# A routing table ordered by slots instead of by experts, in a fused scan and two-layer expert kernel

## The chip, the cores and the metric

One core of one Trainium2 chip runs the whole program in one launch. The metric is the device time in microseconds of an execution; the number given for a kernel is the median of its runs.

## The reference, cut to what matters

```python
# q, k, v, a_re, a_im: [4, 8, 768, 48]
for t in range(768):                          # complex decay, |a| at most 0.999
    S_re, S_im = ar*S_re - ai*S_im + outer(k[t], v[t]), ar*S_im + ai*S_re
    y[t] = q[t] @ S_re
x = y as [N=3072, D=384]                      # tokens x (heads*48)
# first expert layer, 8 experts, F=1024; only tokens with x @ w_skip > 0
e = argmax(x @ w_gate);  g = softmax(x @ w_gate)[e]
x = x + g * relu(x @ w1[e]) @ w2[e]           # the others keep x
# second expert layer, 8 experts, all tokens, no residual
l = norm(x) @ norm(emb).T / tau;  e = argmax(l);  g = softmax(l)[e]
out = g * relu(x @ w1b[e]) @ w2b[e]
```

## The kernel before, in words

**Stages.** The scan goes over 24 chunks of 128 tokens (`chunk`), some 36 to 250 us after the start. The first expert layer (`moe1`) then computes 8 experts with 256 slots each, the second (`moe2`) 8 experts with at most 448. An expert's part of a layer is: fetch token rows by their numbers (`gather`, an indirect DMA of GpSimd into `xg`, line 1003), transpose them (`x_part`, TensorE line 927, evicted to `x` by ScalarE at 933 and VectorE at 934), first matmul (`h_part`, 958), second (`o_part`, 990), and store the output rows by their numbers (`finish`, indirect DMAs of GpSimd: into `xd` at 1044 in the first layer, into `out` at 1239 in the second).

**The routing table.** A token finds its place in `route`: from its logits VectorE makes a one-hot of the expert, a matmul with `SU` (strictly upper triangle and ones) counts the tokens ahead of it, `cnt` holds the count so far and the expert's base, and the sum is the number of a table row. GpSimd then scatters one row per token into the DRAM table by indirect DMA (line 739). A row has W = 17 floats, 68 bytes: 8 logits, the token's number less N, 8 logits. There are two tables, `tab[0]` and `tab[1]`, called lanes; a row is written in one of them, and the other holds zeros there. In either, a layer has its region, and in the region the rows lie by experts: expert e's slot s is row e*N + s. At the start, GpSimd fills the used part with zeros in eight DMAs (line 799); a slot that stays empty thus reads as token N, whose row in `xd` is zero.

**Reading back.** `slots` (line 764) reads 128 slots of every expert from both lanes: SyncE issues two DMAs (767), one into `ts1f` or `ts2f`, one into `LANE`; VectorE adds the two (768) and, in the first layer, makes the indices `ts1i` (770). Of a row 9 columns are wanted, the number and the layer's logits: 36 bytes. As experts lie apart, each slot of each expert is a piece of its own:

```python
return tab[lane][r*E*N : (r+1)*E*N, :].rearrange("(e r) c -> e r c", e=E)[:, a:b, c0:c1]
```

The reads are: one slot tile of expert 0 alone (`early`, "A") and one more ("E") during the scan; the other seven experts' two slot tiles at the scan's end (`moe1`, "ts" 0 and 1); during the first layer the first two slot tiles of the second ("ts2", "A"), for its first expert; and at the end of the first layer all four again (`moe2`), for the other experts. There the order of the experts is found on the chip, by how many tokens they have: `select` (1153) picks for the p-th the rows of its expert out of `ts2f` by a multiply with the one-hot `OH` (1158) and a reduction over the experts (1160) into one of three tiles `F2`, and makes the indices `ts2i` (1161).

**Order.** `Plan` writes each engine's instructions in an order of its own: a list scheduler with a cost for each operation, due times, and dependences by keys (the lists `r` and `w`). An engine works through its queue in that order, SyncE and GpSimd with their DMAs too, and an instruction that waits holds those behind it. After a DMA the planner counts its flight and a charge on top, `more`: for a read of the table 1.2 us. The early reads are ordered behind the scatters that they need by keys.

Of the kernel before, what the change touches and what calls it, by code (L numbers as in the profile page):

```python
# [9 lines left out]
F32 = mybir.dt.float32  # L10
# [268 lines left out]
def kernel(  # L279
# [41 lines left out]
    F2 = [cp.tile([P, 4, E + 1], F32, name=f"F2{i}") for i in range(3)]  # L321
    wrs = cp.tile([P, NPR, 113], F32, name="wrs")
# [4 lines left out]
    LANE = cp.tile([P, E * 4, E + 1], F32, name="LANE")  # L327
# [251 lines left out]
    def chunk(k):  # L579
# [13 lines left out]
        def half(hh):  # L593
# [3 lines left out]
            def w_():  # L597
# [6 lines left out]
                [("ps", hh)], [("wm", k % 2, hh)], D0 - 2)  # L604
# [50 lines left out]
        if ui == UN[u] - 1:  # L655
# [15 lines left out]
            if u == LATE_U - 1:  # L671
                slots(ts1, lambda x: x[:, 1:2, :], lambda lane: region(lane, 0, P, 2 * P)[0].rearrange("p (o c) -> p o c", o=1),
                      sum(tabs, []) + [("tabB", lane) for lane in range(2)], ("ts", "E"), d2 + 4)
            plan.bias = 0.0

    def reserve(c, slots):
# [3 lines left out]
            cnt[:, c : c + 1], pb, float(c * N + slots), ident[:, 0:1], ALU.max, ALU.mult), [("ps7", 3)], ["cnt"])  # L680
# [3 lines left out]
    def route(nm, n, nr, lg, klg, sel, ksel, c0, pay, kpay, inval, pcol, due, late=(), pt0=0):  # L684
# [51 lines left out]
        dve(C, lambda: V.tensor_tensor(cc, cc, cn, op=ALU.add), [k("cn")], ["cnt"])  # L736
        for i in range(n):
# [4 lines left out]
                [("ix", nm)] + klg + kpay + span(["ti"], range(2), (0, E // 2), [lane]), [("tab", nm, i)] + ([("tabB", lane)] if late else []), due, (f"t{lane}", "all"), 1.3, 1.2)  # L742
# [835 lines left out]
```

## Time and profile before

| | |
|---|---|
| median of 3 runs | 703.61 us (701.12 to 706.31) |
| profiled execution, its own time | 706.19 us |
| its span from first to last instruction | 704.3 us |
| mean granted clock of TensorE | 0.958 of full speed |
| TensorE busy (matmuls) | 622.6 us, 88% of the span, 4740 instructions |
| VectorE, ScalarE, GpSimd busy | 459.5, 403.1 and 189.9 us |
| DMA packets | 52007, of them 22909 under 512 bytes |

All rows come from one profiled execution. PE is TensorE's matmuls, PEld its weight loads, DVE is VectorE, ACT ScalarE, POOL GpSimd, SP SyncE; PEq or SPq is an engine's queue. A line as L958 is a line of the kernel; x stands for a count. What stands in brackets in a timeline is the time in which the engine was idle just before the instruction, and what ended it. Times in rows are microseconds from the start of the span, lengths microseconds.

### The profile page before, as it was taken

How to read it: one execution, taken by the hardware profiler on the slowest of the kernel's cores; microseconds unless marked ns; L12 is line 12 of the kernel's file. 1: busy time of each engine (PE TensorE's matmuls, PEld its weight loads, DVE VectorE, ACT ScalarE, POOL GpSimd, SP SyncE). 2: the span in 40 equal slices, each digit the busy share in tenths (PEclk: the TensorE clock that was granted, in tenths of full speed). 3: DMA queues.
4: the chain of work that ended last, by engine and by line, in shares of the span. 5: the costliest groups of instructions: out<-in, count | busy, mean ns of one | idle time of the engine just before them, and what ended most of it. 6: DMA issues, size and time to landing. Idle time of an engine off the chain costs nothing.

```text
span 704.3 us, 12899 instructions
## 1 busy us (share of the span) xinstructions
PE 622.6 (88%) x4740; PEld 599.5 (85%) x4740; DVE 459.5 (65%) x1058; ACT 403.1 (57%) x695; POOL 189.9 (27%) x221
## 2 busy tenths in 40 slices
PE   0088979999979996899999999849999999999994
PEld 0088978889969985899999999749999999999994
DVE  4989888899875553667776657528755636365240
ACT  6977895987856542555555434027553545545340
POOL 5111011025536226122232033443140412111101
PEclk9997898999989999799999999959999999999998
DMA  9858579899556877666554231494653434123001
GB/s 271 315 161 253 204 139 287 251 207 217 127 142 161 271 238 235 209 201 216 167 157 124 87 108 24 84 336 157 226 195 106 148 113 136 37 89 119 23 10 36
DMA packets 52007, 115.91 MB, mean 165 GB/s; under 512 B 22909, under 2 KB 27139, under 8 KB 49250
## 3 DMA queue, kind: packets, MB, share of 16 engines
q1 hardware_dynamic: 41282, 84.50, 38.9%
q0 software_dynamic: 10656, 30.53, 16.1%
q8 instruction: 39, 0.64, 0.4%
q14 instruction: 30, 0.25, 0.1%
HBM read 83.30 MB, written 14.09 MB: 138 GB/s over the span
## 4 chain that ended last, share of the span: by engine, by line
PE 66%; issue 10%; DMA 9%; DVE 6%; ACT 4%; POOL 2%; another core or an unknown queue 1%; SPq 1%; POOLq 0%; DVEq 0%; ACTq 0%
PE PS L958 25%; PE PS L990 24%; PE PS L599 3%; DMA ST<-QK 3%; PE PS L626 3%; PE PS L927 3%; PE PS L436 2%; DMA xd<-XT 2%; PE PS L635 2%; PE PS L646 2%; POOL tab L739 1%; DMA LANE<-tab 1%; PE PS L1061 1%; PE PS L610 1%
## 5 line engine op out<-in xcount | busy, mean ns | idle before, releaser
L990 PE MATMUL PS<-w,h 128*128 128x384 f32 (+1 forms) x1032 | 190.7, 339 | 0.9 <-ACT h L962 0.9
L958 PE MATMUL PS<-x,w 128*128 128x256 f32 (+4 forms) x1152 | 183.3, 317 | 0.0
L990 PEld LDWEIGHTS PS<-w,h 128*128 128x128 f32 (+1 forms) x1032 | 176.2, 184 | 4.1 <-ACT h L962 1.2
L958 PEld LDWEIGHTS PS<-x,w 128*128 128x128 f32 x1152 | 174.9, 194 | 2.1 <-issue 0.4
L962 ACT ACTIVATE h<-PS 128x256 fp32r<-128x256 f32 (+5 forms) x136 | 58.1, 428 | 102.9 <-PE PS L958 92.1
L966 DVE SCALAR_TENSOR_TENSOR h<-PS,h 128x256 fp32r<-128x256 f32 (+4 forms) x184 | 67.4, 390 | 58.7 <-ACT h L962 54.4
L1239 POOL DMA_INDIRECT out<-o,ts2i x30 | 29.9, 997 | 169.7 <-ACT o L1233 123.4
L908 DVE TENSOR_TENSOR w<-r,w 128x768 fp32r<-128x768 f32 x64 | 58.8, 950 | 10.9 <-ACT w L907 7.4
L934 DVE TENSOR_TENSOR x<-PS,x 128x256 fp32r<-128x256 f32 (+4 forms) x48 | 22.6, 484 | 59.4 <-ACT x L933 46.9
L933 ACT CAST x<-PS 128x256 fp32r<-128x256 f32 (+4 forms) x48 | 19.7, 427 | 70.8 <-PE PS L927 49.0
L599 PE MATMUL PS<-ST 96*128 96x128 f32 x384 | 55.1, 291 | 5.4 <-DVE WM L602 3.0
L902 DVE TENSOR_TENSOR w<-r,w 128x1024 fp32r<-128x1024 f32 x45 | 53.3, 1222 | 6.6 <-ACT w L901 5.4
L907 ACT CAST w<-r 128x768 fp32r<-128x768 f32 x64 | 51.0, 833 | 9.5 <-PE PS L990 4.4
L599 PEld LDWEIGHTS PS<-ST 96*128 96x128 f32 x384 | 49.0, 201 | 8.2 <-DVE WM L602 3.6
L436 PE MATMUL PS<-cst 128*128 128x128 f32 x308 | 47.6, 301 | 5.8 <-DVE cs L816 4.3
L436 PEld LDWEIGHTS PS<-cst 128*128 128x128 f32 x308 | 43.3, 214 | 6.7 <-DVE cs L816 4.4
L739 POOL DMA_INDIRECT tab<-LG,ixa x24 | 33.8, 1407 | 47.2 <-DVE ixa L731 13.1
L602 DVE TENSOR_TENSOR WM<-PS,cst 128x512 f32<-128x512 f32 x48 | 32.3, 680 | 20.8 <-PE PS L599 15.3
L901 ACT CAST w<-r 128x1024 fp32r<-128x1024 f32 x45 | 44.6, 1048 | 0.3 <-DMA r<-in_w1a 0.3
L546 POOL DMA_DIRECT2D ST<-QK x50 | 25.4, 516 | 68.6 <-DVE QK L534 66.7
L1003 POOL DMA_INDIRECT xg<-xd,ts2i x30 | 33.1, 1104 | 34.5 <-PE PS L958 10.6
L1044 POOL DMA_INDIRECT xd<-o,ts1i x16 | 17.4, 1088 | 91.5 <-DVE o L1041 59.4
(210 smaller groups left out, 985.2 us busy)
## 6 DMA issues: line engine op xcount, KB each, us to landing
r<-in_w1a SPq DMA_DIRECT2D x24, 512.0 KB
r<-in_w2a SPq DMA_DIRECT2D x32, 384.0 KB
r<-in_w1b SPq DMA_DIRECT2D x24, 512.0 KB
r<-in_w2b SPq DMA_DIRECT2D x32, 384.0 KB
RI<-in_ri SPq DMA_DIRECT2D x6, 1152.0 KB
QK<-in_qk SPq DMA_DIRECT2D x6, 1152.0 KB
ST<-PR SPq DMA_DIRECT2D x12, 432.0 KB
ST<-QK POOLq DMA_DIRECT2D x12, 432.0 KB
```

What stands on the lines that cost most here:

```text
L436: nc.tensor.matmul(PS[7][:, 384:512], lhsT=ident, rhs=maskT, start=True, stop=True)
L599: nc.tensor.matmul(wt[:, h % 4, :], lhsT=st(1, h), rhs=st(0, h), start=True, stop=True)
L739: pool(0.2, lambda i=i, lane=lane: nc.gpsimd.indirect_dma_start(out=tab[lane][:, :], out_offset=IO(ap=ix[:, i : i + 1].bitcast(U32), axis= ...
L901: act(F, lambda s=s: nc.scalar.copy(T["w1"][q % 2][0][s], T["r1"][q % 2][s]), [("r1", q % 2, j), "L"], [k + (0,)])
L902: dve(F, lambda s=s: nc.vector.tensor_tensor(T["w1"][q % 2][1][s], T["r1"][q % 2][s], T["w1"][q % 2][0][s].bitcast(F32), op=ALU.subtract), ...
L907: act(2 * DM, lambda s=s: nc.scalar.copy(T["w2"][0][s], T["r2"][s]), [("r2", j)], [k + (0,)])
L908: dve(2 * DM, lambda s=s: nc.vector.tensor_tensor(T["w2"][1][s], T["r2"][s], T["w2"][0][s].bitcast(F32), op=ALU.subtract), [("r2", j), k + ...
L958: nc.tensor.matmul(ph, lhsT=l, rhs=r, start=(i == 0), stop=(i == len(seq) - 1))
L962: act(w, lambda f=f, ph=ph: nc.scalar.activation(T[name][:, f, o0 : o0 + w], ph, AF.Relu), [("ps", f % 3), "w" if name == "hA" else "L"], ...
L966: dve(b - a, lambda f=f, ph=ph, a=a, b=b, o=o: nc.vector.scalar_tensor_tensor(T[name][:, f, o : o + b - a], ph[:, a - c0 : b - c0], 0.0, T ...
L990: nc.tensor.matmul(po if n == P else po[0 : 2 * stride], lhsT=x, rhs=w[:, f, :], start=(f == 0 and i == 0), stop=(f == NF - 1 and i == len ...
L1003: pool(0.6, lambda: nc.gpsimd.indirect_dma_start(out=T["xg"][s][0:n, :], out_offset=None, in_=xd[0:rows, :], in_offset=IO(ap=idx.bitcast(U ...
```

## The change

The table's rows are ordered by slots: slot s of expert e is row s*8 + e of its layer's region, so that the eight experts' rows of one slot lie together, 8 x 68 = 544 bytes. Slot numbers are multiplied by 8 throughout: in `SU`, the counts, the bases, the limits and the capacities; `SU` takes one multiply more for it.

The reads of 128 slots take whole rows of a slot, all 17 columns: 544 bytes for the second layer (`slots2`), 476 (seven experts) for the first. `LANE` and `ts2f` have 17 columns for it; `LANE` shares its memory with the routing weights `wrs`, and in the first layer both lanes are read into it. Only the two reads of expert 0 alone in the scan keep pieces of 36 bytes (`slots1`, into the new `LE`). The add takes the 9 wanted columns. `select` works on the same number of elements at another step. The three `F2` tiles lie in the columns of the causal mask `maskT`, with a new key "mask" between the mask's readers and the reductions; the matmuls that keep TensorE's clock up (`warm`) read the identity instead. The zero fill writes contiguous runs (1088 and 1904 bytes for each of 64 partitions). The planner's charge after a read is 0.8 us instead of 1.2.

The diff, without lines that only change an index or an offset in the same way:

```diff
-    F2 = [cp.tile([P, 4, E + 1], F32, name=f"F2{i}") for i in range(3)]
-    wrs = cp.tile([P, NPR, 113], F32, name="wrs")
+    F2 = [maskT[:, 4 * (E + 1) * i : 4 * (E + 1) * (i + 1)].rearrange("p (t c) -> p t c", t=4) for i in range(3)]
+    lane = cp.tile([P, E * 4 * W], F32, name="lane")
+    wrs = lane[:, 0 : NPR * 113].rearrange("p (a c) -> p a c", a=NPR)
...
-    LANE = cp.tile([P, E * 4, E + 1], F32, name="LANE")
+    LANE = lane.rearrange("p (i c) -> p i c", c=W)
+    LE = cp.tile([P, 2, E + 1], F32, name="LE")
...
-            nc.tensor.matmul(PS[7][:, 384:512], lhsT=ident, rhs=maskT, start=True, stop=True)
+            nc.tensor.matmul(PS[7][:, 384:512], lhsT=ident, rhs=ident, start=True, stop=True)
...
-                [("ps", hh)], [("wm", k % 2, hh)], D0 - 2)
+                [("ps", hh), "mask"], [("wm", k % 2, hh)], D0 - 2)
...
-                slots(ts1, lambda x: x[:, 1:2, :], lambda lane: region(lane, 0, P, 2 * P)[0].rearrange("p (o c) -> p o c", o=1),
-                      sum(tabs, []) + [("tabB", lane) for lane in range(2)], ("ts", "E"), d2 + 4)
+                slots1(1, P, sum(tabs, []) + [("tabB", lane) for lane in range(2)], ("ts", "E"), d2 + 4)
...
-        dve(C, lambda: V.tensor_tensor(cc, cc, cn, op=ALU.add), [k("cn")], ["cnt"])
+        dve(C, lambda: V.scalar_tensor_tensor(cc, cn, float(E), cc, ALU.mult, ALU.add), [k("cn")], ["cnt"])
...
-    def region(lane, r, a, b, c0=None, c1=None):
-        c0, c1 = (r * E, r * E + E + 1) if c0 is None else (c0, c1)
-        return tab[lane][r * E * N : (r + 1) * E * N, :].rearrange("(e r) c -> e r c", e=E)[:, a:b, c0:c1]
-
-    def slots(t, view, src, ks, key, due, kf=()):
-        parts = [view(x) for x in t["l"]]
+    def region(lane, r, a, b):
+
+        return tab[lane][r * E * N : (r + 1) * E * N, :].rearrange("(s e) c -> s e c", e=E)[a:b]
+
+    def slots(f, parts, src, i, ks, key, due, kf=()):
+
         for lane in range(2):
-            dma(0.2, lambda lane=lane: nc.sync.dma_start(parts[lane], src(lane)), ks, [(key, lane), *kf], due, (f"t{lane}", "read"), more=1.2)
-        dve(math.prod(parts[0].shape[1:]), lambda: nc.vector.tensor_tensor(view(t["f"]), parts[0], parts[1], op=ALU.add), [(key, 0), (key, 1)], [(key, 2), *kf], due)
-        if t is ts1:
-            dve(16, lambda: nc.vector.tensor_scalar(view(t["i"]), view(t["f"])[..., t["c"] : t["c"] + 1], float(N), None, ALU.add), [(key, 2)], [key], due)
-
-    def slot_tiles(nm, n):
-        t = {"f": cp.tile([P, n, E + 1], F32, name=f"{nm}f"), "c": 0 if nm == "ts2" else E}
-        t["l"] = [t["f"], LANE[:, 0:n]]
-        for x in t["l"] if nm == "ts2" else ():
-            nc.gpsimd.memset(x, 0.0)
+            dma(0.2, lambda lane=lane: nc.sync.dma_start(parts[lane], src(lane)), ks, [(key, lane), *kf], due, (f"t{lane}", "read"), more=0.8)
+        o = E if i is None else 0
+        x, y = (p[..., o : o + E + 1] for p in parts)
+        dve(math.prod(f.shape[1:]), lambda: nc.vector.tensor_tensor(f, x, y, op=ALU.add), [(key, 0), (key, 1)], [(key, 2), *kf], due)
+        if i is not None:
+            dve(16, lambda: nc.vector.tensor_scalar(i, f[..., E : E + 1], float(N), None, ALU.add), [(key, 2)], [key], due)
+
+    def slots1(c, a, ks, key, due):
+
+        f = ts1["f"][:, c * E : c * E + 1]
+        slots(f, (f, LE[:, c : c + 1]), lambda lane: region(lane, 0, a, a + P)[:, 0:1, 0 : E + 1], ts1["i"][:, c * E : c * E + 1], ks, (key[0], key[1]), due)
+
+    def slots2(t, n, key, due):
+        f, x = (x[0:n, t * E : t * E + E] for x in (ts2["f"], LANE))
+        slots(f[..., E:], (f, x), lambda lane: region(lane, 1, t * P, t * P + n), None, sum(tabs, []), key, due, [("F", t)])
+
+    def slot_tiles(nm, n, w):
+        t = {"f": cp.tile([P, n, w], F32, name=f"{nm}f")}
...
-        for r, e, lane in itertools.product((0, 1), (0, E // 2), range(2)):
-            n = (CAP1, CAP2)[r] // 64
-            pool(0.4, lambda r=r, e=e, lane=lane, n=n: nc.gpsimd.dma_start(
-                region(lane, r, 0, 64 * n, 0, W)[e : e + E // 2].rearrange("e (p j) c -> p e j c", p=64),
-                zero[:, 0 : E // 2 * n * W].rearrange("p (e j c) -> p e j c", e=E // 2, j=n)), [("S", 0)], [("ti", r, e, lane)], due)
-        dve(P, lambda: nc.vector.tensor_tensor(SU[:, 0], maskT, ident, op=ALU.subtract), (), ["su"], due)
-        dve(P, lambda: nc.vector.tensor_copy(SU[:, 1], ones), (), ["su"], due)
+        for r, x, lane in itertools.product((0, 1), (0, 1), range(2)):
+            n = E * (CAP1, CAP2)[r]
+            part = tab[lane][r * E * N : r * E * N + n, :].rearrange("(x p j) c -> x p (j c)", x=2, p=64)[x]
+            pool(0.4, lambda part=part: nc.gpsimd.dma_start(part, zero[:, 0 : part.shape[1]]), [("S", 0)], [("ti", r, x, lane)], due)
+        dve(P, lambda: nc.vector.tensor_tensor(SU[:, 0], maskT, ident, op=ALU.subtract), ["mask"], ["su"], due)
+        dve(P, lambda: nc.vector.tensor_scalar(SU[:, 0], SU[:, 0], float(E), None, ALU.mult), (), ["su"], due)
+        dve(P, lambda: nc.vector.tensor_scalar(SU[:, 1], ones, float(E), None, ALU.mult), (), ["su"], due)
...
-    ts1, ts2 = slot_tiles("ts1", E * NT1), slot_tiles("ts2", E * 4)
+    ts1, ts2 = slot_tiles("ts1", E * NT1, E + 1), slot_tiles("ts2", E * 4, W)
+    nc.gpsimd.memset(ts2["f"], 0.0)
...
-            slots(ts1, lambda x, t=t: x.rearrange("p (e t) c -> p e t c", e=E)[:, 1:, t, :],
-                  lambda lane, t=t: region(lane, 0, t * P, (t + 1) * P)[1:].rearrange("e p c -> p e c"),
-                  sum(tabs, []), ("ts", t), M0 - 5)
+            f, *x = (x[:, o + t * E + 1 : o + (t + 1) * E] for x, o in ((ts1["f"], 0), (LANE, 0), (LANE, nt * E)))
+            slots(f, x, lambda lane, t=t: region(lane, 0, t * P, (t + 1) * P)[:, 1:], ts1["i"][:, t * E + 1 : (t + 1) * E], sum(tabs, []), ("ts", t), M0 - 5)
...
-                        slots(ts2, lambda x, a=a: x.rearrange("p (e t) c -> p e t c", e=E)[:, :, a],
-                              lambda lane, a=a: region(lane, 1, a * P, a * P + P).rearrange("e p c -> p e c"),
-                              sum(tabs, []), ("ts2", "A", a), due + 20, [("F", a)])
+                        slots2(a, P, ("ts2", "A", a), due + 20)
...
-        src, tmp = (x.rearrange("p (e t) c -> p t c e", e=E)[:, 2 * h : 2 * h + 2] for x in (ts2["f"], LANE))
+        src, tmp = (x.rearrange("p (t e) c -> p t c e", e=E)[:, 2 * h : 2 * h + 2, E:] for x in (ts2["f"], LANE))
         f, V = F2[p % 3][:, 2 * h : 2 * h + 2], nc.vector
         oh = OH[:, p, :].rearrange("p (a b e) -> p a b e", a=1, b=1).to_broadcast([P, 2, E + 1, E])
         dve(250, lambda: V.tensor_tensor(
             tmp, src, oh, op=ALU.mult), kin + [("oh2", min(p, 1))], [("tmp", h)], due)
-        dve(240, lambda: V.tensor_reduce(f, tmp, axis=AX.X, op=ALU.add), kin + [("tmp", h)], [("f2", p % 3, h)], due)
+        dve(240, lambda: V.tensor_reduce(f, tmp, axis=AX.X, op=ALU.add), kin + [("tmp", h)], [("f2", p % 3, h), "mask"], due)
...
-        slots(ts1, lambda x: x[:, 0:1, :], lambda lane: region(lane, 0, 0, P)[0].rearrange("p (o c) -> p o c", o=1),
-              sum(tabs[:3], []), ("ts", "A"), M0 - 20)
+        slots1(0, 0, sum(tabs[:3], []), ("ts", "A"), M0 - 20)
...
-            slots(ts2, lambda x, t=t, n=n: x.rearrange("p (e t) c -> p e t c", e=E)[0:n, :, t, :],
-                  lambda lane, t=t, n=n: region(lane, 1, t * P, t * P + n).rearrange("e p c -> p e c"),
-                  sum(tabs, []), ("ts2", t), M1 - 5, [("F", t)])
+            slots2(t, n, ("ts2", t), M1 - 5)
...
-    cf[:, -P:] = i + P
+    cf[:, -P:] = E * (i + P)
     w8[:] = np.arange(E, 0, -1)
-    base = np.arange(2 * E) * N
+    base = np.concatenate([np.arange(E), E * N + np.arange(E)])
     first[0] = [*base, BIG]
     bia[:] = [math.log(2e-6), SHIFT, -SHIFT, math.pi / 2]
-    lims[:] = base + np.repeat([CAP1, 0], E)
+    lims[:] = base + np.repeat([E * CAP1, 0], E)
     ulim[:] = [U_MAX if g in SQA else U_MAX * U_MAX for g in range(B * TH) for _ in PARTS.get(g, (0,))]
     iota[:] = np.arange(E)
-    caps[:] = CAPS
+    caps[:] = E * np.array(CAPS)
```

## Rows read from the trace of the kernel before

**Rows 1.** The page's chain that ended last, by engine.

```profile
PE 66%; issue 10%; DMA 9%; DVE 6%; ACT 4%; POOL 2%; another core or an unknown queue 1%; SPq 1%; POOLq 0%; DVEq 0%; ACTq 0%
```

**Rows 2.** Busy time (xcount): PE, PEld, DVE, ACT, POOL; clock, DMA, GB/s.

```profile
250.00:292.00 42.00, 32.97 (x233) 31.59 (x231) 20.91 (x74) 17.48 (x40) 18.99 (x18) 0.88 0.78 232
...
292.00:427.00 135.00, 135.00 (x1000) 134.55 (x998) 90.90 (x204) 70.83 (x131) 31.59 (x30) 1.00 0.48 147
...
427.00:490.00 63.00, 50.64 (x343) 48.33 (x343) 37.18 (x167) 21.40 (x60) 27.65 (x31) 0.86 0.53 159
...
490.00:704.30 214.30, 204.84 (x1151) 197.62 (x1149) 104.92 (x257) 101.38 (x207) 40.97 (x41) 0.99 0.31 105
```

**Rows 3.** Waits, 436 to 470: sum, count, longest.

```profile
ACT x L933 <- remote: 17.6, 1, 17.6
...
PE PS L927 <- DVE x L934: 11.0, 1, 11.0
```

**Rows 4.** Timeline of SyncE, scan's end: start, us, issue.

```profile
232.81 0.43 SPq L1195 DMA_DIRECT2D o<-in_cf  x1
...
261.62 3.02 SPq L767 DMA_DIRECT2D LANE<-tab  x1
```

**Rows 5.** Chain of waits, scan's end: start, us, what.

```profile
259.88 5.36 DMA LANE<-tab
```

**Rows 6.** Busy time by stretch, columns as in rows 2.

```profile
262.00:264.00 2.00, 1.90 (x16) 1.71 (x16) 0.17 (x1) 0.53 (x2) 0.00 (x0) 1.00 1.15 178
...
440.00:442.00 2.00, 2.00 (x14) 2.00 (x13) 0.17 (x1) 0.00 (x0) 0.00 (x0) 1.00 0.81 42
```

**Rows 7.** Timeline of GpSimd, scan's end: start, us, instruction, idle before, releaser.

```profile
260.90 0.98 POOL L1044 DMA_INDIRECT xd<-o,ts1i  x1 [4.22 <-DVE o L1041]
...
266.78 1.04 POOL L1003 DMA_INDIRECT xg<-xd,ts1i  x1 [4.91 <-DVE ts1g L1188]
...
280.47 1.00 POOL L1003 DMA_INDIRECT xg<-xd,ts1i  x1 [0.30 <-issue]
```

**Rows 8.** Timeline of ScalarE, scan's end.

```profile
282.71 0.65 ACT L933 CAST x<-PS 128x256 fp32r<-128x256 f32 x2 [3.57 <-remote]
```

**Rows 9.** Chain of waits between the expert layers.

```profile
434.60 2.13 DMA tab<-LG,ixb
...
441.02 3.27 DMA LANE<-tab
```

**Rows 10.** Timeline of SyncE's queue between the layers.

```profile
436.75 2.49 SPq L767 DMA_DIRECT2D ts2f<-tab  x4
...
439.35 3.07 SPq L767 DMA_DIRECT2D LANE<-tab  x4
```

**Rows 11.** Timeline of VectorE between the layers.

```profile
445.31 0.16 DVE L1161 TENSOR_SCALAR ts2i<-F 128x2 int32<-128x2 f32 x1
```

**Rows 12.** Timeline of GpSimd between the layers.

```profile
444.44 1.03 POOL L1239 DMA_INDIRECT out<-o,ts2i  x1 [7.58 <-ACT o L1233]
...
448.68 0.97 POOL L1239 DMA_INDIRECT out<-o,ts2i  x1 [3.21 <-DVE gm L1183]
...
449.95 1.05 POOL L1003 DMA_INDIRECT xg<-xd,ts2i  x1 [0.30 <-issue]
...
464.41 1.00 POOL L1003 DMA_INDIRECT xg<-xd,ts2i  x1 [0.31 <-issue]
```

**Rows 13.** Timeline of ScalarE between the layers.

```profile
466.02 0.32 ACT L933 CAST x<-PS 128x192 fp32r<-128x192 f32 x1 [17.62 <-remote]
```

**Rows 14.** Groups by line, VectorE, 436 to 455: busy us, mean ns, idle before.

```profile
L1158 DVE TENSOR_TENSOR LANE<-ts2f,OH 128x144 f32<-128x144 f32 x13 | 5.3, 416 | 0.1
```

**Rows 15.** Timeline of VectorE, the program's start.

```profile
8.00 0.56 DVE L497 SCALAR_TENSOR_TENSOR RI<-RI 128x384 f32<-128x384 f32 x1 [4.05 <-ACT RI L489]
```

**Rows 16.** Timeline of GpSimd in the scan.

```profile
179.09 0.99 POOL L739 DMA_INDIRECT tab<-LG,ixa  x1 [3.42 <-DMA tab<-LG,ixa]
...
209.92 1.01 POOL L739 DMA_INDIRECT tab<-LG,ixa  x1 [9.65 <-DVE ixa L731]
```

More of the change, by code (lines that the diff above doesn't have):

```diff
@@ L741, in route @@
                 in_=pay[:, i, 0:W], in_offset=None, bounds_check=2 * E * N - 1, oob_is_err=False),
-                [("ix", nm)] + klg + kpay + span(["ti"], range(2), (0, E // 2), [lane]), [("tab", nm, i)] + ([("tabB", lane)] if late else []), due, (f"t{lane}", "all"), 1.3, 1.2)
+                [("ix", nm)] + klg + kpay + span(["ti"], range(2), range(2), [lane]), [("tab", nm, i)] + ([("tabB", lane)] if late else []), due, (f"t{lane}", "all"), 1.3, 1.2)
         tabs.append([("tab", nm, i) for i in range(n)])
@@ L1024, in moe1 @@
                 if e and 2 * e + t < NXG:
-                    gather(0, e, t, P, ti[:, e * nt + t, :], [("ts", t)], kx, M0 - 3 + 10 * e)
+                    gather(0, e, t, P, ti[:, t * E + e, :], [("ts", t)], kx, M0 - 3 + 10 * e)
         for t in range(nt):
-            gates(ts1["f"].rearrange("p (e t) c -> p e t c", e=E)[:, 1:, t, 0:E], ts1["g"].rearrange("p (e t) -> p e t", e=E)[:, 1:, t],
+            gates(ts1["f"][:, t * E + 1 : (t + 1) * E, 0:E], ts1["g"][:, t * E + 1 : (t + 1) * E],
                   [("ts", t)], ("g1", 2 + t), M0 + 6)
@@ L1036, in finish @@
             ui = i - i0
-            ox, xs = i % 4, slot(0, e, t)
+            ox, xs, s = i % 4, slot(0, e, t), t * E + e
             kt = ("g1", 2 + t if e else t)
@@ L1041, in finish @@
             dve(448, lambda: nc.vector.scalar_tensor_tensor(
-                T["o"][ox], po, ts1["g"][:, i : i + 1], T["xg"][xs], ALU.mult, ALU.add),
+                T["o"][ox], po, ts1["g"][:, s : s + 1], T["xg"][xs], ALU.mult, ALU.add),
                 kpo + [kt, ("xg", xs)], [("o", ox)], due)
             pool(0.6, lambda: nc.gpsimd.indirect_dma_start(
-                out=xd[:, :], out_offset=IO(ap=ti[:, i, :].bitcast(U32), axis=0),
+                out=xd[:, :], out_offset=IO(ap=ti[:, s, :].bitcast(U32), axis=0),
                 in_=T["o"][ox], in_offset=None, bounds_check=N - 1, oob_is_err=False),
@@ L1101, in moe1 @@
                 if (i - NXG) // 2 == e - 1:
-                    gather(0, i // 2, i % 2, P, ti[:, i, :], [("ts", i % 2)], kx, d)
+                    gather(0, i // 2, i % 2, P, ti[:, i % 2 * E + i // 2, :], [("ts", i % 2)], kx, d)
     def place(final, due):
@@ L1129, in first_expert @@
         dve(E, lambda: V.tensor_scalar(OH[:, 0, :], key, big[:, 0:1], None, ALU.is_equal), ["key", "big"], [("oh2", 0)], d)
-        dve(E, lambda: V.scalar_tensor_tensor(big, OH[:, 0, :], 2.0 * P, lims[:, E : 2 * E], ALU.mult, ALU.add), [("oh2", 0)], ["big"], d)
+        dve(E, lambda: V.scalar_tensor_tensor(big, OH[:, 0, :], 2.0 * P * E, lims[:, E : 2 * E], ALU.mult, ALU.add), [("oh2", 0)], ["big"], d)
         dve(E, lambda: V.tensor_tensor(big, big, pb, op=ALU.max), [("ps7", 6)], ["big"], d)
@@ L1207, in late @@
         dve(1, lambda: nc.vector.scalar_tensor_tensor(
-            ts1["i"][:, 1, :], ob[:, E : E + 1], float(N), ts1["f"][:, 1, E : E + 1], ALU.add, ALU.add),
+            ts1["i"][:, E, :], ob[:, E : E + 1], float(N), ts1["f"][:, E, E : E + 1], ALU.add, ALU.add),
             [("ps7", 4), ("ts", "E")], [("ts", "B")], M0 - 4)
-        gather(0, 0, 1, P, ts1["i"][:, 1, :], [("ts", "B")], kx, M0 - 4)
-        dve(W, lambda: nc.vector.tensor_tensor(ts1["f"][:, 1, :], ts1["f"][:, 1, :], ob, op=ALU.add),
+        gather(0, 0, 1, P, ts1["i"][:, E, :], [("ts", "B")], kx, M0 - 4)
+        dve(E + 1, lambda: nc.vector.tensor_tensor(ts1["f"][:, E, 0 : E + 1], ts1["f"][:, E, 0 : E + 1], ob, op=ALU.add),
             [("ps7", 4), ("ts", "E"), ("ts", "B")], [("ts", "BF")], M0 - 2)
-        gates(ts1["f"][:, 1:2, 0:E], ts1["g"][:, 1:2], [("ts", "BF")], ("g1", 1), M0)
+        gates(ts1["f"][:, E : E + 1, 0:E], ts1["g"][:, E : E + 1], [("ts", "BF")], ("g1", 1), M0)
     def moe2():
```

12 lines of the change are left out of this document (8 added, 4 removed).

## Prediction

> **What bounds the kernel now.** I read the page's chain first: TensorE has 66% of it, so only time in which TensorE stands still can be won [rows 1]. Then the busy time by stage: in the first expert layer TensorE is busy 135.00 of 135 us (292 to 427), and from 490 on 204.84 of 214.30 us. Between these it loses 42.00 - 32.97 = 9.0 us at the scan's end (250 to 292) and 63.00 - 50.64 = 12.4 us between the two expert layers (427 to 490) [rows 2]. The routing table is read back for good in just these two stretches, so they are the ones to read closely. The longest waits of the kernel sit there too: ScalarE waits 17.6 us at one eviction (L933), and TensorE then 11.0 us for VectorE's half of it [rows 3].
>
> The scan's end: SyncE issues the four reads of the table; the second goes out at 259.88, and the fourth holds the queue for 3.02 us, where a 128-row read of the same kind (`o<-in_cf`, 512 bytes a row) took 0.43 [rows 4, 5]. The second read is 5.36 us on its way, to 265.24 [rows 5]. In 262 to 264 the DMA engines are full (1.15) and move 178 GB/s; with the second layer's table alone, 440 to 442, they are 0.81 busy for 42 GB/s [rows 6]: the 36-byte pieces fill the engines without moving much. GpSimd's store of the first expert's rows, issued at 260.90, shares them. The first gather of the next experts' rows starts at 266.78, the eleventh and last of the burst at 280.47 [rows 7]. ScalarE's eviction of the first transposes, which needs only the first two gathers, starts at 282.71 [rows 8], 1.2 us after the burst's end (280.47 + 1.00).
>
> Between the layers: the last scatter into the table takes 2.13 us to land, the reads go out from 436.75 to 442.42 (2.49 us for the first four, 3.07 for the other lane's), and the third read of the second lane is 3.27 us on its way, to 444.29 [rows 9, 10]. VectorE has the first index at 445.31 + 0.16 = 445.5 [rows 11]. GpSimd does not use it then: its written order has the store of the second output tile first, which waits for ScalarE until 448.68; the first gather is at 449.95, the twelfth ends at 465.41 [rows 12], and ScalarE's eviction starts at 466.02 [rows 13], 0.6 us later. So both times TensorE resumes when the burst of gathers is over. Why, the trace does not say (the releaser is "remote"); I count on it as a regularity seen twice.
>
> **The change part by part.** *Fewer, longer pieces.* A full read of the second layer is 128 x 8 = 1024 pieces of 36 bytes, then 128 of 544; of the first layer 128 x 7 = 896, then 128 of 476. I price the new reads by bounds: an issue 0.43 us, as `o<-in_cf` [rows 4]; a landing at least 2.13 us after its issue, the scatter's, at most as before, 5.36 and 3.27 [rows 5, 9].
>
> At the scan's end I take 3.0 us for the second read, nearer the lower end since the pieces that fill the engines are gone but weights still move: ready at 259.88 + 3.0 = 262.9, that is 2.4 us sooner (bounds 0 and 3.2). The store that GpSimd issued at 260.90 meets fewer pieces too. The first gather then comes about 2.3 us sooner, the burst ends 2.3 us sooner, and TensorE, idle for it, resumes 2.3 us sooner. The next stage has no idle TensorE time [rows 2], so this is kept: **-2.3**.
>
> Between the layers, eight issues of 0.43 from 436.75, the second lane's from 438.3, land the table by about 438.3 + 4 x 0.43 + 2.13 = 442.1; the second lane's first two, on which the first index hangs, by 438.3 + 0.86 + 2.13 = 441.3. VectorE's multiply, reduction and conversion and the add in front of them, about 0.4 each (a multiply is 0.416 [rows 14]), give the index at 443.0, against 445.5. By itself that is worth nothing, for GpSimd's store still stands first and waits to 448.68. But the planner that writes the order now charges 0.8 us instead of 1.2 behind each read, so it sees the index 0.4 us sooner and may put the gathers ahead of that store. I take it that it does, a little likelier than not: the planner gives GpSimd what it believes ready first, and in the trace the two are ready within 3.2 us (445.5 and 448.68). Then the first gather follows the first store, at 444.44 + 1.03 + 0.3 = 445.8, instead of 449.95: 4.2 sooner; the second store falls inside the burst and lengthens it by 1.3; TensorE resumes 4.2 - 1.3 = **2.9** sooner.
>
> *Cost on VectorE.* The multiplies and reductions of `select` keep 144 elements; only their step changes, from 144 bytes to 68. No row has that step. Bounds for one: 0.2 (the conversion's 0.16 and a bit) and 0.8, twice 0.416 [rows 14]; I take 0.416 unchanged. Four gathers need two such pairs and take 4 x 1.3 us on GpSimd, so even the upper bound hides behind GpSimd, but for 0.8 us on the way to the first index. That the three `F2` tiles now lie in the mask's columns, with the key "mask", puts the reductions in the order in which they are written down; they run on one engine anyway: 0.
>
> *Small parts.* One more multiply on `SU` falls into the 4.05 us in which VectorE waits for ScalarE before 8.00 [rows 15]: 0, or 0.3 without that cover. The zero fill keeps its eight issues on GpSimd; its pieces fall from 2048 to 512 while the first loads run, but TensorE's first work comes out of ScalarE and VectorE there: 0, between -0.5 and 0. Wider memset for `ts2f`, none for `LANE`: the same elements. The two one-column reads (`slots1`) keep 36-byte pieces, 128 of them: 0. The early reads of the second layer's first two slot tiles feed gathers that are used a whole expert later: 0. The scatters' rows now lie 544 bytes apart; no row prices that, I take 0, at most 1 us on the 2.13 of the last one.
>
> Sum: 2.3 + 2.9 = 5.2 us. The profiled execution took 706.19 us (span 704.3 and 1.9 around it), which gives 701.0; the median of the three runs is 2.6 lower, so on it **703.6 - 5.2 = 698.4 us**. A change of under 1% (7.0 us) is about what cannot be told from none here.
>
> **The rivals.** *One transition pays alone.* The order on GpSimd between the layers stays: 703.6 - 2.3 = 701.3. For it: the planner looks 0.4 us ahead only, and I cannot see its margin. Or only the second pays, 700.7: the first layer's pieces are 476 bytes and may stay slow. The Trainium skill, page "DMA: Bandwidth & Descriptors", section "Specifications", says line rate needs at least 512 bytes; by it alone 544 passes and 476 does not, and the sum would be 2.9 instead of 5.2. What [rows 6] show is engines filled by number of pieces at 36 bytes each, and 476 bytes means seven times fewer; no row here has 476-byte reads.
>
> *Nothing pays: 703.6.* TensorE is released by something else than the burst's end, for instance the weight loads that run beside both bursts, and the earlier gathers only wait longer.
>
> *It pays more: 690.* If the first eviction gets through before the burst chokes it, the idle stretch between the layers, 11.0 us [rows 3], goes almost whole: 703.6 - 2.3 - 11.0 = 690.3. Against it: with gathers sooner and TensorE's own work before them ending at the same time, the transposes come later within the burst, not earlier.
>
> *Slower: 711.* The planner writes the whole order anew from the changed charges and the "mask" key. GpSimd's queue in the scan holds scatters into the table and the copies that feed the scan (`ST<-QK`) in one line. A scatter that waits for its indices holds the copies behind it; such waits are 3.42 us at 179.09 and 9.65 at 209.92 [rows 16]. If one of the long kind is put ahead of copies that TensorE lacks, the price is 9.65, and the time 703.6 - 2.3 + 9.65 = 711.0; with one of 3.42, 704.7. It decides once the wait exceeds the 2.3 to 5.2 gained.
>
> **How the numbers follow.** Forecast 0.38; one transition alone 0.22; nothing 0.08; more 0.14; slower order 0.18. The range 692.5 to 708 holds the first three (0.68) and about a third of the other two. Faster by over 1% (under 696.6): the 0.14, and the third of the forecast in which its terms come near their bounds, 0.26. Slower by over 1% (over 710.6): two thirds of the slow case, 0.12. The rest, 0.62, is within 1%.
>
> **What would show it.** In the changed profile: reads of the table with issues near 0.4 us and no 3 us one; the DMA share at 262 to 264 and 438 to 444 well down; the first gather near 264.5; between the layers a gather ahead of the second output store, at about 443.5 (all 2.3 earlier), the burst ending near 460, and the eviction within 1.3 us of its end in both places. It is wrong if the gathers come sooner and the eviction does not, or if GpSimd's order keeps the store first; and if TensorE's idle time in the scan, 36 to 250, changes by more than 3 us, the order decided and not the pieces.

## The result, and the profile after

The changed kernel takes 698.29 us (median of 13 runs), the kernel before 706.31 in as many: 8.0 us less by the medians, 6.0 by the means, a ratio of 0.9915, with a 95% interval from 0.9887 to 0.9942. This ratio and those below are of the means of the runs, without the few that are over 1.5% above their kernel's fastest (here one of 3397 us of the kernel before). The forecast was 698.4 us, 5.2 less than the 703.6 of the first three runs, a ratio of 0.9926. The size of the gain is right; that 698.4 and 698.29 agree to 0.1 us is luck, since the median of the kernel before rose by 2.7 us with more runs. The way there is not the one forecast, as the profile shows: its span is 695.8 us against 704.3, and what was gained lies for the most part in a stage for which the forecast had nothing.

These runs, and the two profiles of before and after, come from one chip. The experiments ran on three others, where the kernel before takes 685 to 687 us. Each of their ratios is against the kernel before on the same chip. On the first chip itself layout and order were not run apart.

The two profiles, one execution of each, step by step, from rows of the timelines (each row is the time between two events, so that the shift of all that comes earlier drops out):

| stretch | before | after | difference |
|---|---|---|---|
| start to the last chunk's score matmul | 245.86 | 236.65 | -9.2 |
| on to the first of the four reads of the table | 13.54 | 16.37 | +2.8 |
| on to the first gather of the burst | 7.38 | 6.42 | -1.0 |
| on to ScalarE's first eviction | 15.93 | 16.01 | +0.1 |
| on to the first read between the layers | 154.04 | 153.52 | -0.5 |
| on to the first gather there | 13.20 | 9.49 | -3.7 |
| on to ScalarE's eviction there | 16.07 | 19.06 | +3.0 |
| on to the end of the span | 238.3 | 238.3 | 0 |

The timeline of TensorE at the last chunk's score matmul, first before, then after:

```profile
245.86 1.15 PE L646 MATMUL PS<-wrs,XTT 128*128 128x113 f32 x8
```

```profile
236.65 1.15 PE L648 MATMUL PS<-lane,XTT 128*128 128x113 f32 x8
```

SyncE's four reads of the first layer, after (timeline), and the second of them in the chain of waits:

```profile
253.02 3.17 SPq L768 DMA_DIRECT2D lane<-tab  x4
```

```profile
254.92 3.41 DMA lane<-tab
```

Against [rows 4, 5]: the reads are issued 0.33 to 0.43 us each, the one of 3.02 is gone, and the second is 3.41 us on its way in place of 5.36. (The four together take 3.17 because the second waits for the last scatter into its lane.) The windows, with the columns of [rows 2], at the reads of either layer: the DMA engines are 0.91 busy for 261 GB/s where [rows 6] had 1.15 for 178, and 0.42 for 101 where it had 0.81 for 42. So far the reads did what was expected of them; how much of that is the layout's doing is seen below.

```profile
256.00:258.00 2.00, 1.90 (x17) 1.71 (x16) 0.17 (x1) 0.53 (x2) 0.00 (x0) 1.00 0.91 261
432.00:434.00 2.00, 2.00 (x13) 2.00 (x12) 0.78 (x3) 0.39 (x1) 0.00 (x0) 1.00 0.42 101
```

The chain of waits, after: an early read of the table, and the scatter behind it on GpSimd.

```profile
239.56 4.58 DMA LE<-tab
...
244.94 0.39 POOL tab L740
```

GpSimd after, at the scan's end and between the layers (timeline; compare [rows 7, 12]):

```profile
244.94 1.00 POOL L740 DMA_INDIRECT tab<-LG,ixa  x1 [6.73 <-DVE ts1i L773]
...
254.80 0.98 POOL L1053 DMA_INDIRECT xd<-o,ts1i  x1 [2.73 <-DVE o L1050]
259.44 1.05 POOL L1013 DMA_INDIRECT xg<-xd,ts1i  x1 [3.66 <-DVE h L976]
...
272.55 1.13 POOL L1013 DMA_INDIRECT xg<-xd,ts1i  x1 [0.31 <-issue]
...
437.18 0.97 POOL L1247 DMA_INDIRECT out<-o,ts2i  x1 [8.11 <-ACT o L1241]
438.46 1.05 POOL L1013 DMA_INDIRECT xg<-xd,ts2i  x1 [0.30 <-issue]
...
451.75 1.03 POOL L1247 DMA_INDIRECT out<-o,ts2i  x1 [0.16 <-issue]
...
454.41 1.01 POOL L1013 DMA_INDIRECT xg<-xd,ts2i  x1 [0.30 <-issue]
```

The second output store stands behind ten gathers now: the planner did turn the two round. ScalarE's evictions behind the bursts, after (compare [rows 8, 13]):

```profile
275.45 0.65 ACT L943 CAST x<-PS 128x256 fp32r<-128x256 f32 x2
...
457.52 0.54 ACT L943 CAST x<-PS 128x192 fp32r<-128x192 f32 x2 [16.37 <-remote]
```

Both come after the burst's end again, 1.8 us (272.55 + 1.13) and 2.1 us (454.41 + 1.01).

### The profile page after: what moved, and what is told of

Its sections match the earlier page's. It is cut to its first block, busy times and chain, and to the rows that moved or that the text cites. A ratio compares the mean times of both kernels' runs of the same rounds, so it can differ in the third digit from the quotient of the medians.

```text
span 695.8 us, 12914 instructions
## 1 busy us (share of the span) xinstructions
PE 620.8 (89%) x4748; PEld 598.9 (86%) x4748; DVE 459.7 (66%) x1059; ACT 402.5 (58%) x695; POOL 186.6 (27%) x220
## 4 chain that ended last, share of the span: by engine, by line
PE 69%; DMA 9%; ACT 6%; DVE 5%; issue 4%; another core or an unknown queue 3%; POOL 2%; SPq 0%; POOLq 0%; DVEq 0%; ACTq 0%
PE PS L1000 26%; PE PS L968 26%; DMA ST<-QK 4%; PE PS L601 4%; PE PS L628 3%; DMA tab<-LG,ixa 3%; PE PS L937 2%; PE PS L637 2%; PE PS L648 2%; ACT L381 1%; PE PS L1070 1%; POOL tab L740 1%; PE PS L612 1%; DMA RI<-in_ri 1%
## 5 line engine op out<-in xcount | busy, mean ns | idle before, releaser
L1000 PE MATMUL PS<-w,h 128*128 128x384 f32 (+1 forms) x1032 | 193.0, 342 | 2.8 <-ACT h L972 2.8
L438 PE MATMUL PS<-cst 128*128 128x128 f32 x316 | 49.3, 304 | 3.3 <-DVE w8s L731 2.2
L438 PEld LDWEIGHTS PS<-cst 128*128 128x128 f32 x316 | 44.8, 216 | 4.4 <-DVE w8s L731 2.6
L740 POOL DMA_INDIRECT tab<-LG,ixa x24 | 30.6, 1276 | 38.4 <-DMA tab<-LG,ixa 14.2
```

Source lines behind the costliest of these rows:

```text
L438: nc.tensor.matmul(PS[7][:, 384:512], lhsT=ident, rhs=ident, start=True, stop=True)
L740: pool(0.2, lambda i=i, lane=lane: nc.gpsimd.indirect_dma_start(out=tab[lane][:, :], out_offset=IO(ap=ix[:, i : i + 1].bitcast(U32), axis= ...
L1000: nc.tensor.matmul(po if n == P else po[0 : 2 * stride], lhsT=x, rhs=w[:, f, :], start=(f == 0 and i == 0), stop=(f == NF - 1 and i == len ...
```

## The experiments

**Layout and order taken apart.** The change does two things to the program: the table's layout, and the instruction order that the planner writes from its new charge, keys and operations. Two kernels have one of each; the orders are the same on all engines as in the kernel that they are taken from.

Layout alone:

```diff
# the changed kernel, with the planner's inputs of the kernel before
-            ... (f"t{lane}", "read"), more=0.8)
+            ... (f"t{lane}", "read"), more=1.2)
-                [("ps", hh), "mask"], [("wm", k % 2, hh)], D0 - 2)
+                [("ps", hh)], [("wm", k % 2, hh)], D0 - 2)
# "mask" dropped in select and consts too; both operations on SU[:, 0] in one planned step
```

> The changed kernel with the instruction order of the kernel before on every engine (charge 1.2, no mask key in the planner, the extra multiply on SU joined to its neighbour). If the gain of the changed kernel sits in the order of the scan: the last chunk's score matmul starts near 246 us as before (237 in the changed kernel), the reads at the scan's end land about 2.4 us sooner after their issue (3.4 us on the way instead of 5.4 to 5.8), between the layers the second output store still stands ahead of the gathers, and the whole gains 2 to 3 us (ratio 0.996 to 0.997). If the layout carries the gain: ratio 0.991 to 0.993, near the changed kernel's 0.9915.

Measured: 1.0019 (0.9984 to 1.0055). The layout alone gains nothing that can be measured; both expectations had it faster, by 0.3% at the least.

Order alone:

```diff
# the kernel before, with the planner's inputs of the changed kernel
-            ... (f"t{lane}", "read"), more=1.2)
+            ... (f"t{lane}", "read"), more=0.8)
# "mask" added to the same keys, and one more multiply on SU[:, 0], by 1.0
```

> The kernel before, table by experts and pieces of 36 bytes, with the instruction order of the changed kernel on every engine. If the order of the scan decides: the last score matmul starts near 237 us, then about 2.4 us are lost again at the scan's end and about 1 us between the layers, where the first gather waits for the index; the whole gains 4 to 6 us (ratio 0.992 to 0.994). If the forecast's own account holds (order worth only 2.9 us, between the layers, the scan unchanged): last score matmul at 246, ratio 0.996. If the layout carries it: ratio 0.998 to 1.002.

Measured: 0.9870 (0.9817 to 0.9923), more than any of the three had it; last score matmul at 238.6 us.

The charge alone, in the kernel before:

```diff
-            ... (f"t{lane}", "read"), more=1.2)
+            ... (f"t{lane}", "read"), more=0.8)
```

> The kernel before with one number changed: the planner's charge behind a read is 0.8 us instead of 1.2. The planner writes a third order. If any new order of the scan moves the end by several microseconds either way: the last score matmul moves by more than 2 us from 246 and the time with it, sign open. If the charge alone is what made the changed kernel's order good: last score matmul near 237, ratio 0.992 to 0.995. If order hardly matters: 245 to 247 and ratio 0.996 to 1.002.

Measured: 0.9882 (0.9845 to 0.9918). The last score matmul is at 243.8 in its profile, so the mark named for it failed, and the time fell by more than the 0.5 to 0.8% expected with that mark; but the profiled execution is the slowest of its twelve runs (682.55 us, median 676.19). Its queue on GpSimd has the two places studied below as the changed kernel has them.

The changed kernel beside these three:

> The changed kernel itself on the same chip as the three, to compare with: ratio 0.989 to 0.994.

Measured: 0.9883 (0.9831 to 0.9936). So one number of the planner, with the old table and its 36-byte pieces, buys what the whole change buys.

**The kernel before on another chip.**

> The kernel before, looked at again beside the others. In the first profiles (of before and of the changed kernel) ScalarE's eviction after each burst of gathers came only when the burst was over; in the four profiles of the first set of experiments it came after two to six gathers. If that is a matter of the execution or the chip and not of the kernel, this profile shows the eviction between the layers some 5 us after the first gather (not 16), and a span near 684 to 688 us; if it is the kernel's, 704.

Measured: one run of 680.5 us, span 678.7, shorter still than expected. Its timelines of GpSimd and ScalarE between the layers:

```profile
434.19 1.09 POOL L1003 DMA_INDIRECT xg<-xd,ts2i  x1 [0.30 <-issue]
```

```profile
439.04 0.78 ACT L933 CAST x<-PS 128x192 fp32r<-128x192 f32 x2 [6.40 <-PE PS L927]
```

The same program's eviction comes 4.9 us after the first gather, in the middle of the burst, and TensorE is named as what released it; on the first chip it came after 16.1 us, released by "remote" [rows 12, 13]. The transposes that it waits for were not late there. TensorE's timeline, the kernel before on the first chip, then on the other:

```profile
454.45 0.73 PE L927 MATMUL PS<-cst,xg 64*128 64x64 f32 x3 [0.99 <-DMA xg<-xd,ts2i]
```

```profile
438.73 0.74 PE L927 MATMUL PS<-cst,xg 64*128 64x64 f32 x3 [0.98 <-DMA xg<-xd,ts2i]
```

On the first chip they end at 455.2 and the eviction starts 10.8 us later; on the other it starts while they still run. At the scan's end it starts 9.5 us after the first gather there, and 15.9 on the first chip. The profiles of the three other chips all lie at 4.6 to 7.8 us between the layers and at 7.3 to 11.1 at the scan's end, and name TensorE. The release at the burst's end, on which the forecast counted, belongs to the first chip, not to the kernel.

**Why the faster reads pay nothing.** At the scan's end, the run with the layout alone: its index on VectorE, its queue on GpSimd, and the DMA issues of 250 to 265 us (what, queue, count, KB each where it is known, median us from issue to landing):

```profile
260.80 0.17 DVE L773 TENSOR_SCALAR ts1i<-ts1f 128x7 int32<-128x7 f32 x1
```

```profile
257.30 0.98 POOL L1056 DMA_INDIRECT xd<-o,ts1i  x1 [5.26 <-DVE o L1053]
263.48 1.05 POOL L1016 DMA_INDIRECT xg<-xd,ts1i  x1 [5.19 <-DVE inv L1033]
```

```profile
lane<-tab SPq DMA_DIRECT2D x4, 59.5 KB, 4.7
...
xd<-o,ts1i POOLq DMA_INDIRECT x1, 5.4
```

The index is there at 261.0, and the gather starts at 263.5, 0.8 us after the landing of the store of the first expert's rows (257.3 + 5.4 = 262.7). The kernel before on another chip, in the same two views:

```profile
254.63 0.98 POOL L1044 DMA_INDIRECT xd<-o,ts1i  x1 [4.43 <-DVE o L1041]
259.83 1.05 POOL L1003 DMA_INDIRECT xg<-xd,ts1i  x1 [4.22 <-DVE h L966]
```

```profile
ts1f<-tab SPq DMA_DIRECT2D x2, 31.5 KB, 5.3
LANE<-tab SPq DMA_DIRECT2D x2, 31.5 KB, 5.0
```

```profile
xd<-o,ts1i POOLq DMA_INDIRECT x1, 4.4
```

Again 0.8 us after the landing, at 259.0. (The reads, 4.7 against 5.0 to 5.3, gained less than the first pair of profiles made believe: in the new order SyncE issues the second read 1.9 us behind the first, and that shortens its way too. With the order alone, still in 36-byte pieces, the second read is 3.81 us on its way, against 4.96 in the kernel before on the other chip.) The store writes into `xd` and the gathers read from it, both by row numbers that only the chip knows; the planner marks the two as a clash over the whole of `xd` (`"all"` against `"read"`), although the rows belong to different experts. So the gathers wait for the landing as well as for the index, and sooner indices only move the wait. Of the ten profiles that show this landing eight have the gather 0.7 to 0.8 us behind it. In the other two, the charge alone and the last run below, both with the old table, the gather follows the index by 0.28 us and comes some 1.3 and 0.8 us later than the landing alone would have let it: there shorter reads could have paid up to that much. Between the layers it is GpSimd's first output store that stands ahead. Order alone, where the pieces are still of 36 bytes:

```profile
431.69 0.97 POOL L1240 DMA_INDIRECT out<-o,ts2i  x1 [8.11 <-DVE F L1161]
433.44 1.05 POOL L1004 DMA_INDIRECT xg<-xd,ts2i  x1 [0.78 <-issue]
```

The gather follows the store after 0.78 us; in the changed kernel it is 0.30. The reads gain at most this 0.48 us there: with the charge alone, also in 36-byte pieces, it is 0.30 as well.

**The two places on GpSimd's queue.** First the output store, moved by itself, in the kernel before and back again in the changed one (GpSimd's queue; all other queues stay):

```diff
 DMA out<-o,ts2i              # the first output store
-DMA out<-o,ts2i              # the second
 DMA xg<-xd,ts2i x6
 CAST WE<-rk
 DMA xg<-xd,ts2i x4
 CAST WE<-rk
+DMA out<-o,ts2i
```

> The kernel before with one instruction moved in GpSimd's queue: between the layers the second output store stands behind ten gathers instead of ahead of them; every other queue is as before. The forecast's account of this place: first gather up to 4.2 us sooner, less about 1, 2.9 us won (ratio 0.996). Where the gathers wait for the index as well (the slow reads of the table by experts): 1 to 2 us (0.997 to 0.9985). If all of the order's gain lay here and none in the scan: ratio 0.987 to 0.990.

Measured: 0.9980 (0.9942 to 1.0019), by itself not to be told from nothing. The other way round:

> The changed kernel with that one instruction put back: the second output store ahead of the gathers, all else as changed. If the scan's order carries the gain: ratio 0.990 to 0.993, some 3 us slower than the changed kernel (0.988 beside the same set of runs earlier). If the place between the layers carries it: 0.998 to 1.002.

Measured: 0.9951 (0.9908 to 0.9994), between the two expectations, against 0.9883 for the changed kernel itself on the chip of the first runs. The intervals overlap. The windows of 427 to 490 us, columns as in [rows 2], of this run and of the changed kernel on another chip:

```profile
427.00:490.00 63.00, 60.13 (x362) 56.29 (x361) 42.79 (x140) 29.01 (x62) 26.53 (x29) 0.97 0.66 238
```

```profile
427.00:490.00 63.00, 62.32 (x383) 58.50 (x382) 44.15 (x143) 33.20 (x74) 29.51 (x32) 1.00 0.68 244
```

With the store ahead TensorE is busy 2.2 us less, and the granted clock, 0.97 over these 63 us, is at its lower level (1.2 GHz) for some 4 us of them.

All profiles of the other chips show the place more clearly than the times do. From the first read between the layers to the end of the span the four with the store ahead take 256.4 to 259.8 us, the eight with it behind the gathers 251.2 to 254.3, in the means 4.8 us less.

Then the scan. In the second profile of the kernel before TensorE waits for copies of GpSimd (timelines of TensorE and of GpSimd; the copies `ST<-QK` bring the features of the seventh group):

```profile
195.09 0.74 PE L610 MATMUL PS<-cst,ST 96*128 96x96 f32 x3 [2.34 <-DMA ST<-QK]
196.77 0.42 PE L610 MATMUL PS<-cst,ST 96*128 96x96 f32 x1 [0.95 <-DMA ST<-QK]
```

```profile
188.60 1.10 POOL L546 DMA_DIRECT2D ST<-QK  x2
190.94 1.07 POOL L739 DMA_INDIRECT tab<-LG,ixa  x1 [1.23 <-DMA tab<-LG,ixa]
...
192.56 0.53 POOL L546 DMA_DIRECT2D ST<-QK  x1
193.40 1.17 POOL L739 DMA_INDIRECT tab<-LG,ixa  x1 [0.30 <-issue]
194.55 1.03 POOL L546 DMA_DIRECT2D ST<-QK  x2
```

The changed kernel has the five in one piece, on another chip at 184.37:

```profile
184.37 2.58 POOL L548 DMA_DIRECT2D ST<-QK  x5
```

The edit, in the kernel before:

```diff
+DMA ST<-QK x5
 DMA tab<-LG,ixa
-DMA ST<-QK x2
 DMA tab<-LG,ixa
 DMA VT<-in_v
-DMA ST<-QK
 DMA tab<-LG,ixa
-DMA ST<-QK x2
```

> The kernel before with five of GpSimd's copies (ST<-QK, the second half of the features of the seventh scan group) moved ahead of three scatters into the table, as they stand in the changed kernel; every other queue is as before. In the second profile of the kernel before TensorE waits 2.3 and 1.0 us for these copies near 195 us and its clock is then halved for 6.8 us. If that is where the new order wins in the scan: no wait of TensorE for ST<-QK and no halved clock between 188 and 205, the last score matmul 3 to 6 us sooner than the 240 to 246 of the kernels with the old order, ratio 0.991 to 0.996. If the gain of the scan is spread over the whole order: ratio 0.998 to 1.002.

Measured: 0.9957 (0.9924 to 0.9991). The time came out, its marks did not: TensorE still waits (1.23 and 1.10 us), the clock is still 0.83 in 188 to 208 us, and the last score matmul is at 244.5. The copies come at 191.99 only, behind two scatters of 3.18 and 3.36 us that stand there in the old order too. So where the 0.4% comes from is not shown. Both edits together:

> The kernel before with both edits of GpSimd's queue, the five copies ahead of three scatters in the scan and the second output store behind ten gathers between the layers. If these two places are what the new order wins: ratio 0.985 to 0.991, as the whole new order in the old layout (0.987). If they are only part of it: 0.992 to 0.997.

Measured: 0.9906 (0.9868 to 0.9944). That is near the whole order (0.9870), with overlapping intervals, but the scan's share is not won in the new order's way: the last score matmul is at 244.4, and in this profile the gain lies behind the first read between the layers, 252.0 us to the end against 258.3.

The windows of 188 to 208 us, in the second profiles of before and of the changed kernel: TensorE 15.38 us busy at a granted clock of 0.83, against 19.52 at 1.00.

```profile
188.00:208.00 20.00, 15.38 (x133) 14.12 (x129) 15.58 (x41) 11.77 (x17) 9.67 (x12) 0.83 0.54 131
```

```profile
188.00:208.00 20.00, 19.52 (x216) 17.89 (x214) 19.95 (x50) 18.85 (x31) 3.69 (x6) 1.00 0.61 157
```

The last score matmul of all profiles says the same more roundly. With the old order on TensorE, six profiles: 239.6 to 245.9, mean 243.6; with the changed kernel's, seven profiles: 235.3 to 239.2, mean 237.1. The 9.2 us of the first pair is 6.5 in the mean.

Where the new order wins them can be read off the score matmuls. The last six span 29.4 to 30.0 us in every profile; the stretch just ahead, from the seventh last to the sixth last, differs (TensorE, second profiles of before and of the changed kernel):

```profile
191.36 1.15 PE L646 MATMUL PS<-wrs,XTT 128*128 128x113 f32 x8 [0.66 <-DVE LG L652]
...
209.93 1.07 PE L646 MATMUL PS<-wrs,XTT 128*128 128x113 f32 x8
```

```profile
197.24 1.15 PE L648 MATMUL PS<-lane,XTT 128*128 128x113 f32 x8
...
207.00 1.12 PE L648 MATMUL PS<-lane,XTT 128*128 128x113 f32 x8
```

It takes 17.9 to 19.4 us in the six profiles of the old order, and 9.8 to 10.6 in the seven of the new and in that of the charge alone. Up to there the new order is 2.4 us behind in the mean. Here TensorE idles 4.0 us at a granted clock of 0.82 in the kernel before, 0.3 at 1.00 in the changed one, and 3.0 at 0.81 with the copies moved: that edit left most of the loss where it was.

Two profiles of one order differ too, and that goes with TensorE's clock. The windows of 60 to 84 us, first and second profile of the kernel before:

```profile
60.00:84.00 24.00, 22.51 (x183) 21.90 (x184) 20.14 (x25) 18.32 (x23) 3.01 (x6) 0.72 0.75 206
```

```profile
60.00:84.00 24.00, 20.94 (x237) 19.57 (x237) 24.00 (x31) 21.57 (x28) 3.01 (x6) 1.00 0.81 237
```

In both TensorE had waited 2.49 us just before a score matmul at 61.5 and 61.6 us. In the first the clock then was at its lower level for some 13 us, in the second it was not, and the next score matmul came at 82.6 against 78.5. Over 36 to 250 us the six profiles of the old order have granted clocks of 0.97 (last score matmul 239.6), 0.95 (241.5) and four times 0.94 (244.4 to 245.9).

**A shorter burst.** GpSimd's copy of one column holds the later gathers until ScalarE has evicted the first transposes; at the scan's end the second gather of the second expert is also moved forward, to stand behind the first.

```diff
 DMA xg<-xd,ts1i x4
+COPY hold<-x 128x1           # reads what ScalarE evicts first
 DMA xg<-xd,ts1i
...
 DMA xg<-xd,ts2i x6
+COPY hold<-x 128x1
 CAST WE<-rk
```

> The changed kernel with two pauses in GpSimd's queue: a one-column copy of the first transposed tile holds back the gathers behind the fourth (scan's end) and the sixth (between the layers) until ScalarE has made the first eviction. If TensorE's results are released only when a burst of gathers is over, as both first profiles read: the evictions come within 2 us of the fourth and sixth gather, 7 and 10 us sooner than in the first profile of the changed kernel, ratio 0.963 to 0.975. If the release has nothing to do with GpSimd's burst: no gain, the later gathers come some 3 us later, ratio 0.988 to 0.995.

Measured: 0.9785 (0.9745 to 0.9825), the fastest kernel of the study by its ratio, and between the two expectations. But it ran on a chip that does not hold TensorE's results back, so it tells nothing of the first chip; there the pauses stay untried. The moved gather without the pauses:

> The changed kernel with one gather moved: at the scan's end the two gathers of the second expert's rows follow each other, in place of standing first and third; no pause. If the kernel with pauses (0.9785) owed its extra gain to this order, since the transposes need just these two gathers: 0.979 to 0.984, the first eviction about 2 us sooner after the first gather (9.5 in the changed kernel's second profile, 8.0 with the pauses). If it owed it to the pauses: 0.986 to 0.990.

Measured: 0.9844 (0.9798 to 0.9890). The eviction comes 7.3 us after the first gather, 8.0 with the pauses and 9.5 in the changed kernel. In these profiles the moved gather thus gives all of the gain at the scan's end; whether the pauses add anything, the overlapping intervals leave open. And the same in the old layout:

> The kernel before, table by experts, with the changed kernel's order and the two pauses and the moved gather of the run with pauses. If the layout is worth nothing also where the burst no longer hides it: within 0.4% of the run with pauses (0.9785). If its shorter reads count there: 0.983 to 0.986, some 3 to 5 us slower than that run.

Measured: 0.9806 (0.9761 to 0.9850). Here too the layout is worth nothing that can be told from zero.

## Why the forecast came out

The time was right by luck, since its two terms were not: on the first chip they came to about a third of the 5.2 us (1.0 less 0.1 at the scan's end, 0.7 between the layers), and the scan, which stood at nothing, made up for them with 9.2 less 2.8.

*The pieces, as transfers: right in their marks, half right in their cause.* Issues of 0.33 to 0.43 at the scan's end and 0.33 to 0.58 between the layers against the 0.43 forecast; the second read 3.41 us on its way against 3.0. But with the order held, the read at the scan's end lands 0.3 to 0.6 us sooner, not 2.4, and those between the layers 0.7 to 1.1 (medians of 1.9 to 2.1 against 2.6 to 3.2). The second lane's start, 438.3 in the forecast, is 436.75 + 4 x 0.43 = 438.5 by its own price; nothing hangs on the 0.2. The Trainium skill, page "DMA: Bandwidth & Descriptors", section "Specifications", wants at least 512 bytes for line rate, which the 544-byte rows pass and the 476-byte ones do not; the runs do not contradict it, but no run here has both sizes at one place.

*The scan's end, -2.3: failed at the step "the first gather then comes about 2.3 us sooner".* It came 1.0 sooner after the reads. On the other chips it waits for the landing of the store that GpSimd issued before; the two profiles of the first chip do not show that landing, but there too the gather starts 1.0 and 0.6 us behind the index, not 0.28. The forecast saw that store, but only as something that shares the DMA engines. The trace had a sign of it: in the chain of waits (the line below) VectorE had the index at 265.59 + 0.17 = 265.8, and the gather began at 266.78 [rows 7]. On top of that the new order put the early read of the last slot tile 2.4 us behind the last score matmul in place of 0.8 ahead of it; the scatters behind wait for that read (4.58 us on its way, in the chain above; 6.73 us of GpSimd at 244.94), and 2.8 us were given back. The transposes, too, need not the first two gathers, as the forecast read it: in the changed kernel the two stand first and third.

```profile
265.59 0.17 DVE ts1i L770
```

*Between the layers, -2.9: right as an order, lost on the first chip.* The planner did put the gathers ahead of the store, and the first came 3.7 us sooner after the reads (4.2 forecast). But the burst now holds that store as a thirteenth entry, and on that chip the eviction came 2.1 us after its end in place of 0.6: 3.0 of the 3.7 were given back, 0.7 kept. On the other chips the store's place was worth 0.2% (by itself), 0.5% (on top of the copies) and 0.7% (in the changed kernel), 1.4 to 4.7 us, and 4.8 us by the stretches of the profiles; the 2.9 lies among them, though the intervals are wide and the first includes no gain at all. The halved clock behind the wait is part of it.

*VectorE, SU, zero fill: right as far as rows show it.* The multiplies of `select` take 414 ns against 416 [rows 14], the reductions 395 against 400. Of `SU` and the zero fill nothing can be seen: the first score matmul is at 62.2 us with the layout alone, at 61.3 to 62.4 in the five profiles of the old table with that order.

*The rival "slower: the planner writes the whole order anew" named what decided, with the sign turned.* It held that a long scatter could be put ahead of copies that TensorE lacks. It is the order before in which TensorE waits for such copies behind long scatters, and the new one in which it does not; that they alone decide is not shown. With the old layout the order alone is worth 1.3%, with the old order the layout alone nothing that can be measured, so the order decided and not the pieces. The forecast's own test for that did not see it: TensorE's idle time from 36 to 250 us is 16.6 us before and 18.2 after, a change of 1.6 where it had asked for more than 3, while the last score matmul moved by 9.2. The two runs apart show it, not that mark.

What stays open: which differences of the order win the 6.5 us of the scan, since the five copies by themselves do not; why the clock falls in one profile of a program and not in another; what the layout alone is worth on the first chip; and what holds TensorE's results back there.

## What to carry to other kernels

Where an order comes from a planner, a change of a transfer's size is also a change of order, and the two have to be run apart: here, on the other chips, reads with seven to eight times fewer pieces paid nothing that could be measured, and the constant edited beside it paid all. Before a wait is priced, list everything that the waiting instruction waits for: a gather that starts 0.8 us after a store's landing gains nothing from a faster index. A regularity seen twice in one trace can be that chip's: look at the same program on another. And a total that agrees with the forecast proves none of its terms.

## What the runs showed of the hardware

One chip held TensorE's results back until a burst of GpSimd's gathers was over and others did not, with the same program: 16.1 against 4.9 us from the first gather to the eviction between the layers (10.8 us of them behind the end of the transposes), 15.9 against 9.5 at the scan's end. This rests on two profiles of the first chip and twelve of the others. The two differences, 11.2 and 6.4 us, are most of the 20 us by which the kernel before is slower there (706 against 685 to 687).

TensorE's granted clock differed between two executions of one program: 0.72 and 1.00 in 60 to 84 us of the kernel before on two chips, with the score matmul behind it at 82.6 and 78.5 us.
